# Attention into a feed-forward block: q of batch 1 loaded four tokens to a partition and turned by DMA

## The chip, the cores and the metric

The kernel runs on one core of a Trainium2 chip. The metric is the device time of one execution in microseconds (us). A core has a matrix engine (TensorE, in the profile PE, its weight loads PEld), a vector engine (VectorE, DVE), an engine for activation functions (ScalarE, ACT), a general one (GpSimd, POOL) and one that issues transfers (SyncE, SP). Transfers are carried by 16 DMA engines; POOL issues them on queue q0, SP on queue q1. Tiles lie in SBUF; PE writes to PSUM.

## The reference

Linear attention with a cosine weighting of positions, followed by a feed-forward block with the approximate GELU. q, k and v are 8 batches x 8 heads x 576 tokens x 64, in float32.

```python
def phi(x, c, s):
    r = np.maximum(x, 0.0)
    return np.concatenate([r * c, r * s], axis=-1)   # 64 -> 128 features
q_p, k_p = phi(q, cos_w, sin_w), phi(k, cos_w, sin_w)
kv  = np.einsum('bhsf,bhsd->bhfd', k_p, v)
z   = np.sum(k_p, axis=2)
num = np.einsum('bhsf,bhfd->bhsd', q_p, kv)
den = np.einsum('bhsf,bhf->bhs', q_p, z)[..., None] + 1e-06
x   = (num / den), heads side by side                # 4608 tokens x 512
h   = x @ w_in                                       # 512 x 2048
out = (h * sigmoid(1.702 * h)) @ w_out               # 2048 x 512, float32
```

## The kernel before

The work goes batch by batch. A schedule is written out by hand: each engine works through its instructions in the order of the program, and so do the queues of POOL and SP. A transfer that must wait for its buffer holds up what is issued behind it on its engine.

For one batch the steps are these. `load` brings k and v (and q of batches 0 and 1) as float32 with nine consecutive tokens on a partition and two heads stacked on the partitions (64 partitions each). `load_q` brings q of the other batches with four consecutive tokens on a partition, in two DMAs: 512 tokens on 128 partitions with all heads, and the last 64 tokens on 64 partitions. `trig` (L145 on DVE, L143 on ACT) and `trig_q` (L158) apply the ReLU and the weights of cosine and sine; they write `kr` (k) and `qn0` or `qn` (q, two views of one tile), in bfloat16. q must then be turned so that the 128 features lie on the partitions (`qT`). `qturn_pe` (L174) does it on PE by 128x128 transposes into PSUM, from where `qevac` (L182 on ACT, L184 on DVE) copies them out. `qturn_dma` (L192) does it by a transposing DMA of SP from SBUF to SBUF, one for each of five parts of a batch. `vcopy` (L164, L166) casts v into `vt`, which has a column of ones beside each head for the sum z.

`kv_mm` (L210) computes k^T v with z, `kv_evac` copies it to SBUF, `num_mm` (L223) computes numerators and denominators of 128 tokens, `num_div` (L231, L233, L235 on DVE) divides them into `xn`. x is turned by PE (`xturn_mm` L253, then `xturn_evac` L260 on ACT) in batches 0 and 1 and by DMA (`xturn_dma` L266) from batch 2 on. The PSUM pool of these steps (`at`) has two buffers, which `kv_mm`, `num_mm` and, in batch 1, the turn of q take one after the other; the turn of x writes into the buffer of its numerators, so that a buffer comes free when `xturn_evac` has read it.

The first product (`mm1`, L276) gives 16 blocks of 128 of the 2048 hidden features for 512 tokens, four matmuls each; ACT applies the GELU (L281). The remaining 64 tokens of a batch go through `mm1_tail` (L303) or, for batches 2 to 7 together, `mm1_tails` (L294). The second product (`mm2`, L326) sums over the 16 blocks for a row group of 128 tokens. It is called in parts: `mm2(b, t, lo, hi)` sums blocks lo to hi of row group t; blocks 4g to 4g+3 need the quarter g of w_out. With the last part ACT copies the group out of PSUM (L330) and POOL stores it (L333).

The loads at the start go like this. SP loads k and q of batch 0. POOL loads v of batch 0 and the four parts of w_in, cast to bfloat16 under way, and then k of batch 1, two quarters of w_out, q and v of batch 1 and the other two quarters of w_out. The attention of batch 1 is laid between the parts of the second product of batch 0. From batch 2 on, a loop does the same with the next batch, q turned by DMA.

These functions are touched:

Of the kernel before, what the change touches and what calls it, by code (L numbers as in the profile page):

```python
# [9 lines left out]
F32 = mybir.dt.float32  # L10
BF16 = mybir.dt.bfloat16
# [8 lines left out]
def kernel(  # L20
# [9 lines left out]
    nc = tc.nc  # L30
    B, H, S, D = q.shape
# [4 lines left out]
    NS = S // 64  # L36
    MT = 512
    NI = H // 2
# [7 lines left out]
    pmm = ctx.enter_context(tc.tile_pool(name="pmm", bufs=4, space=PSUM))  # L46
    pat = ctx.enter_context(tc.tile_pool(name="pat", bufs=2, space=PSUM))
# [4 lines left out]
    def raw(name, dt=F32):  # L52
        return one.tile([128, NI, S], dt, name=name)

    def src_of(src, b, i0=0, i1=NI):
        return src[b, 2 * i0:2 * i1].rearrange("(i hh) (p j) d -> (hh p) i (j d)", hh=2, j=NS)

    qf = one.tile([128, 2560], F32, name="qf")
    kf, vf, vb = raw("kf"), raw("vf"), raw("vb", BF16)
    qf0 = qf[:, 0:NI * S].rearrange("p (i e) -> p i e", i=NI)  # L60
    for t, src, cut in ((kf, k, 192), (qf0, q, 256)):
# [34 lines left out]
    qn0 = qn.rearrange("p c h f -> p (c h f)")[:, 0:NS * NI * 128].rearrange(  # L96
        "p (j i f) -> p j i f", j=NS, i=NI)
# [14 lines left out]
    def load(t, src, b, eng=nc.gpsimd):  # L112
        eng.dma_start(out=t, in_=src_of(src, b))

    def load_q(b, eng=nc.sync):
        eng.dma_start(out=qf[:, 0:2048].rearrange("p (h e) -> p h e", h=H),
                            in_=q[b, :, 0:512, :].rearrange("h (p c) d -> p h (c d)", c=4))
        eng.dma_start(out=qf[0:64, 2048:2560].rearrange("p (h e) -> p h e", h=H),
                            in_=q[b, :, 512:S, :].rearrange("h p d -> p h d"))

    def load_win(g):
        nc.gpsimd.dma_start(out=w_in_sb[g], in_=win_r[:, :, ts(g, 512)])

    def load_wout(g):
        nc.gpsimd.dma_start(out=w_out_sb[:, ts(g, 4), :], in_=wout_r[:, g])
# [6 lines left out]
    load_win(1)  # L132
    nc.gpsimd.tensor_copy(gate[0:1, 1:2], vb[0:1, 3, 0:1])
    load_win(2)
    load_win(3)


    def trig(dst, src, j, act=False):
        i = src[:, :, ts(j, 64)]
        for cs, w in enumerate((cosw, sinw)):  # L140
            o = dst[:, j, :, ts(cs, 64)]
            if act:
                nc.scalar.activation(o, i, AF.Relu, scale=w[:, j:j + 1])  # L143
            else:
                nc.vector.tensor_scalar(o, i, 0.0, w[:, j:j + 1], op0=MAX, op1=MUL)  # L145

    def trig_q(c, act=False):
        n = 128 if c < 4 else 64
        if c < 4:
            i = qf[:, 0:2048].rearrange("p (h c d) -> p c h d", h=H, c=4)[:, c]  # L150
        else:
            i = qf[0:64, 2048:2560].rearrange("p (h d) -> p h d", h=H)
        for cs, w in enumerate((cosw, sinw)):
            o, sc = qn[0:n, c, :, ts(cs, 64)], w[0:n, NS + c:NS + c + 1]
            if act:
                nc.scalar.activation(o, i, AF.Relu, scale=sc)
            else:
                nc.vector.tensor_scalar(o, i, 0.0, sc, op0=MAX, op1=MUL)  # L158

    def vcopy(i0, i1, act=False):  # L160
        o = vt[:, :, i0:i1, 0:64].rearrange("p j i e -> p i j e")
        i = vf[:, i0:i1].rearrange("p i (j e) -> p i j e", e=64)
        if act:
            nc.scalar.activation(o, i, AF.Copy)  # L164
        else:
            nc.vector.tensor_copy(o, i)  # L166

    tps = {}

    def qturn_pe(c, home=None):  # L170
        tp = pmm.tile([128, 2, NI, 128], BF16, name="mm") if home is None else home
        for j in range(2 * c, min(2 * c + 2, NS)):
            for i in range(NI):
                nc.tensor.transpose(tp[:, j % 2, i], qn0[:, j, i, :], ident)  # L174
        tps[c] = tp

    def qevac(c, act=False):
        n = min(2 * c + 2, NS) - 2 * c
        o = qT[:, :, ds(c * 128, n * 64)].rearrange("f h (j p) -> f j h p", j=n)
        i = tps.pop(c)[:, 0:n].rearrange("f j i (hh p) -> f j (i hh) p", hh=2)  # L180
        if act:
            nc.scalar.activation(o, i, AF.Copy)  # L182
        else:
            nc.vector.tensor_copy(o, i)  # L184

    def at_homes():
        t = pat.tile([128, 2, 512], F32, name="at")
        return [t[:, u].bitcast(BF16).rearrange("p (j i f) -> p j i f", j=2, i=NI) for u in range(2)]

    def qturn_dma(c):  # L190
        n = 128 if c < 4 else 64
        nc.sync.dma_start_transpose(out=qT[:, :, c * 128:c * 128 + n],  # L192
                                    in_=qn[0:n, c].rearrange("p h f -> p (h f)"))
# [19 lines left out]
    def kv_evac(i0, i1):  # L213
        o = st["kvs"][:, :, i0:i1, 0:65]
        nc.vector.tensor_copy(o, st["ps", i0].rearrange("p hh (i e) -> p hh i e", e=65))  # L215
# [29 lines left out]
    def x_open(b):  # L245
        x[b] = xpool.tile([128, KC, S], BF16, name="xT")

    def xturn_mm(c):
        ps, xn = nums[c]
        xv = xn.rearrange("p a h e -> p (a h e)")  # L250
        for kc in range(KC):
            o = ps[:, kc // 2, ds(264 + (kc % 2) * 64, 64)].bitcast(BF16)
            nc.tensor.transpose(o, xv[:, ts(kc, 128)], ident)  # L253
# [43 lines left out]
    def mm1_tail(b, half):  # L297
        if half == 0 and b % 2 == 0:
            gt[0] = gpool.tile([128, FC, 128], BF16, name="gtail", bufs=2)
        hps = pmm.tile([128, 8, 64], F32, name="mm")  # L300
        for f in range(8):
            for kc in range(KC):
                nc.tensor.matmul(hps[:, f], w_in_of(kc, half * 8 + f), x[b][:, kc, MT:S],  # L303
                                 start=(kc == 0), stop=(kc == KC - 1))
        nc.scalar.activation(gt[0][:, ts(half, 8), ts(b % 2, 64)], hps, AF.Gelu_apprx_sigmoid)

    yp = {}
    out_j = [out[b * S:b * S + S].rearrange("(p j) d -> j p d", j=NS) for b in range(2)]

    def rows(b, t):  # L310

        if t == 4:
            return [(64 * u, 64, out_j[u][NS - 1]) for u in range(2)]
        if t > 4:
            return [(64 * u, 64, out[(w + 1) * S - 64:(w + 1) * S])
                    for u, w in enumerate((TB + 2 * (t - 5), TB + 2 * (t - 5) + 1))]
        if b < 2:
            return [(64 * u, 64, out_j[b][2 * t + u]) for u in range(2)]
        return [(0, 128, out[b * S:b * S + 512].rearrange("(p c) d -> c p d", c=4)[t])]

    def mm2(b, t, lo, hi, c0=0, c1=d_model):
        if lo == 0:
            yp[t, c0] = pmm.tile([128, d_model], F32, name="mm")
        for fc in range(lo, hi):
            w = gT[fc][:, ts(t, 128)] if t < 4 else gt[0][:, fc, :] if t == 4 else gl_t[:, fc, ts(t - 5, 128)]
            nc.tensor.matmul(yp[t, c0][:, c0:c1], w, w_out_sb[:, fc, c0:c1],  # L326
                             start=(fc == 0), stop=(fc == FC - 1))
        if hi == FC:
            ysb = ypool.tile([128, d_model], F32, name="ysb")
            nc.scalar.activation(ysb[:, c0:c1], yp[t, c0][:, c0:c1], AF.Identity)  # L330
            for p0, n, dst in rows(b, t):
                eng = nc.sync if b == B - 1 else nc.gpsimd
                eng.dma_start(out=dst[:, c0:c1], in_=ysb[p0:p0 + n, c0:c1])  # L333
# [81 lines left out]
    start_block(0)  # L415


    load(kf, k, 1)
    load_wout(0)
    load_wout(1)  # L420
    load(qf0, q, 1)
    load(vf, v, 1)
    load_wout(2)
    load_wout(3)
    for j in range(NS):
        trig(kr, kf, j)
# [1 line left out]
        mm1(0, fc)  # L428
    mm1_tail(0, 0)
    mm1_tail(0, 1)  # L430
    for j in range(5):
        trig(qn0, qf0, j)
    for j in range(5, NS):
        trig(qn0, qf0, j, act=True)
    for t in range(4):
        mm2(0, t, 0, 4)
    mm2(0, 0, 4, 8)
    mm2(0, 1, 4, 8)
    ha = at_homes()
    qturn_pe(0, ha[0])  # L440
    qturn_pe(1, ha[1])
    qevac(0)
    qevac(1, act=True)
    mm2(0, 2, 4, 8)
    mm2(0, 3, 4, 8)
    hb = at_homes()
    qturn_pe(2, hb[0])
    qturn_pe(3, hb[1])
    vcopy(0, 2)
    vcopy(2, 4, act=True)  # L450
    qevac(2)
    qevac(3, act=True)
    load_q(2, nc.gpsimd)
    load(kf, k, 2, nc.gpsimd)
    load(vf, v, 2, nc.gpsimd)
    mm2(0, 0, 8, 12)
    mm2(0, 1, 8, 12)
    hc = at_homes()
    qturn_pe(4, hc[0])
    qevac(4)  # L460
    kv_open()
    kv_mm(0, 4, vt_rhs, 0, 65)
    kv_evac(0, 4)
    mm2(0, 2, 8, 12)
    mm2(0, 3, 8, 12)
    num_mm(0)
    num_div(0)
    num_mm(1)
    num_div(1)
    x_open(1)  # L470
    mm2(0, 0, 12, 16)
    mm2(0, 1, 12, 16)
    xturn_mm(0)
    xturn_evac(1, 0)
    mm2(0, 2, 12, 16)
    xturn_mm(1)
    xturn_evac(1, 1)
    num_mm(2)
# [83 lines left out]
```

## Time and profile before

| | |
|---|---|
| median of 3 runs | 295.21 us (295.20 to 295.99) |
| the profiled execution | 295.72 us, its span 294.0 us |
| PE busy | 284.8 us (97%), 2552 instructions |
| DVE, ACT, POOL busy | 126.1, 131.5, 34.7 us |
| TensorE clock granted | 1.00 throughout |
| DMA | 52.38 MB, of it 32.52 MB on q1 (SP) and 19.47 MB on q0 (POOL) |

The busy time of PE is its matmuls and transposes. The share of the DMA is the mean over 16 engines; it can pass 1, where packets of one engine overlap. The chain that ended last is followed back from the last instruction: at each step to what released it, or to the instruction before it on its engine. In the chain's view a row has a start, a length and what ran. The table of windows gives for each stretch of the span the busy time of each engine, the clock and the DMA's share. The DMA view has packets, MB and share of time for each queue, and for each issue the time until its data landed.

### The profile page before, as it was taken

How to read it: one execution, taken by the hardware profiler on the slowest of the kernel's cores; microseconds unless marked ns; L12 is line 12 of the kernel's file. 1: busy time of each engine (PE TensorE's matmuls, PEld its weight loads, DVE VectorE, ACT ScalarE, POOL GpSimd, SP SyncE). 2: the span in 40 equal slices, each digit the busy share in tenths (PEclk: the TensorE clock that was granted, in tenths of full speed). 3: DMA queues.
4: the chain of work that ended last, by engine and by line, in shares of the span. 5: the costliest groups of instructions: out<-in, count | busy, mean ns of one | idle time of the engine just before them, and what ended most of it. 6: DMA issues, size and time to landing. Idle time of an engine off the chain costs nothing.

```text
span 294.0 us, 6250 instructions
## 1 busy us (share of the span) xinstructions
PE 284.8 (97%) x2552; PEld 161.9 (55%) x2587; DVE 126.1 (43%) x362; ACT 131.5 (45%) x230; POOL 34.7 (12%) x68
## 2 busy tenths in 40 slices
PE   8879999999999999999999999999999999999995
PEld 4775656857454555455545554555455545565444
DVE  4674514693264825581567156725763420000000
ACT  7847653685104631463136412651175117773111
POOL 6260031500123001100110011000100010000000
PEclk9999999999999999999999999999999999999999
DMA  7999979596178965797469936995595240000322
GB/s 255 238 222 283 372 192 362 169 139 184 38 139 254 296 182 136 213 311 211 111 199 338 223 90 183 328 221 131 144 371 110 74 116 36 3 0 2 88 90 71
DMA packets 67228, 52.38 MB, mean 178 GB/s; under 512 B 47392, under 2 KB 57376, under 8 KB 67200
## 3 DMA queue, kind: packets, MB, share of 16 engines
q1 hardware_dynamic: 59824, 32.52, 43.2%
q0 software_dynamic: 7376, 19.47, 23.2%
q8 instruction: 20, 0.33, 0.4%
q14 instruction: 8, 0.07, 0.1%
HBM read 36.70 MB, written 9.44 MB: 157 GB/s over the span
## 4 chain that ended last, share of the span: by engine, by line
PE 95%; ACT 1%; issue 1%; DVE 1%; ACTq 0%
PE mm L326 42%; PE mm L276 36%; PE at L210 4%; PE mm L294 4%; PE at L223 3%; PE mm L338 3%; PE mm L303 2%; ACT g L281 1%; PE at L253 1%; DVE xn L235 1%; PE at L174 1%; PE mm L174 1%; DVE inv L233 0%; DVE den L231 0%; ACT ysb L330 0%
## 5 line engine op out<-in xcount | busy, mean ns | idle before, releaser
L326 PE MATMUL mm<-w_out_sb,g 128*128 128x512 bf16 (+1 forms) x506 | 116.2, 372 | 1.3 <-issue 0.2
L276 PE MATMUL mm<-xT,w_in 128*128 128x512 bf16 (+1 forms) x598 | 112.7, 345 | 0.5
L281 ACT ACTIVATE g<-mm 128x512 bf16<-128x512 f32 x128 | 75.6, 598 | 31.9 <-PE mm L276 31.9
L276 PEld LDWEIGHTS <-w_in 128*128 128x128 bf16 x608 | 61.8, 114 | 49.0
L326 PEld LDWEIGHTS <-g 128*128 128x128 bf16 x528 | 48.7, 98 | 49.5
L330 ACT ACTIVATE ysb<-mm 128x512 f32<-128x512 f32 (+1 forms) x37 | 21.7, 586 | 111.4 <-PE mm L326 111.4
L333 POOL DMA_DIRECT2D out_dram<-ysb x38 | 20.7, 548 | 177.2 <-ACT ysb L330 177.1
L145 DVE TENSOR_SCALAR kr<-kf,cosw 128x256 bf16<-128x256 f32 x68 | 23.7, 348 | 27.3 <-DMA kf<-in_k_dram 27.3
L235 DVE TENSOR_TENSOR xn<-at,inv 128x512 bf16<-128x512 f32 x40 | 27.7, 692 | 1.6 <-DVE inv L233 0.2
L145 DVE TENSOR_SCALAR kr<-kf,sinw 128x256 bf16<-128x256 f32 x68 | 23.8, 350 | 0.0
L231 DVE TENSOR_SCALAR den<-at 128x8 f32<-128x8 f32 x40 | 6.7, 166 | 36.9 <-PE at L223 36.9
L215 DVE CAST kvs<-at 128x520 bf16<-128x520 f32 (+1 forms) x9 | 5.8, 642 | 33.1 <-PE at L210 33.0
L223 PEld LDWEIGHTS <-qT 128*128 128x128 bf16 x320 | 14.5, 97 | 7.3
L223 PE MATMUL at<-kvs,qT 128*128 128x65 bf16 x320 | 15.9, 193 | 0.0
L158 DVE TENSOR_SCALAR qn<-qf,sinw 128x512 bf16<-128x512 f32 (+1 forms) x30 | 14.3, 477 | 0.0
L158 DVE TENSOR_SCALAR qn<-qf,cosw 128x512 bf16<-128x512 f32 (+1 forms) x30 | 14.3, 477 | 0.0
L210 PEld LDWEIGHTS <-kr 64*128 64x128 bf16 x648 | 10.2, 94 | 3.5 <-issue 3.2
L294 PE MATMUL mm<-xt,w_in 128*128 128x384 bf16 x64 | 10.6, 326 | 0.0
L326 PE MATMUL mm<-w_out_sb,gl_t 128*128 128x512 bf16 x47 | 10.5, 379 | 0.1
L338 PE MATMUL mm<-warm 128*128 128x64 bf16 (+1 forms) x114 | 8.5, 237 | 1.3 <-DVE warm L76 1.3
L294 PEld LDWEIGHTS <-w_in 128*128 128x128 bf16 x64 | 7.2, 113 | 3.3
L295 ACT ACTIVATE gl_t<-mm 128x384 bf16<-128x384 f32 x16 | 7.9, 491 | 2.4 <-PE mm L294 2.4
(60 smaller groups left out, 122.7 us busy)
## 6 DMA issues: line engine op xcount, KB each, us to landing
kf<-in_k_dram SPq DMA_DIRECT2D x5, 1152.0 KB, 6.5
vf<-in_v_dram SPq DMA_DIRECT2D x5, 1152.0 KB, 9.5
qf<-in_q_dram SPq DMA_DIRECT2D x5, 1024.0 KB, 5.7
out_dram<-ysb POOLq DMA_DIRECT2D x20, 256.0 KB, 2.6
kf<-in_k_dram POOLq DMA_DIRECT2D x2, 1152.0 KB, 10.2
vf<-in_v_dram POOLq DMA_DIRECT2D x2, 1152.0 KB, 13.7
out_dram<-ysb POOLq DMA_DIRECT2D x18, 128.0 KB, 3.2
w_in<-in_moe_w_in_dram POOLq DMA_DIRECT2D x4, 512.0 KB, 9.2
```

The lines of the kernel that those rows point to most:

```text
L145: nc.vector.tensor_scalar(o, i, 0.0, w[:, j:j + 1], op0=MAX, op1=MUL)
L158: nc.vector.tensor_scalar(o, i, 0.0, sc, op0=MAX, op1=MUL)
L210: nc.tensor.matmul(st["kv", i][:, hh, ds(col, n)], kr[r, j, i, :], rhs(r, i, j), start=(j == 0), stop=(j == NS - 1))
L223: nc.tensor.matmul(ps[:, h // 4, ds((h % 4) * 65, 65)], qT[:, h, ts(c, 128)], st["kvs"][:, hh, i, 0:65], start=True, stop=True)
L235: nc.vector.tensor_tensor(xn, pv[:, :, :, 0:64], inv.unsqueeze(3).to_broadcast([128, 2, 4, 64]), op=MUL)
L276: nc.tensor.matmul(hp[fc][:, t0:t1], w_in_of(kc, fc), x[b][:, kc, t0:t1], start=(kc == 0), stop=(kc == KC - 1))
L281: nc.scalar.activation(g, hp.pop(fc), AF.Gelu_apprx_sigmoid)
L294: nc.tensor.matmul(hps, w_in_of(kc, fc), xt[:, kc, :], start=(kc == 0), stop=(kc == KC - 1))
L326: nc.tensor.matmul(yp[t, c0][:, c0:c1], w, w_out_sb[:, fc, c0:c1], start=(fc == 0), stop=(fc == FC - 1))
L330: nc.scalar.activation(ysb[:, c0:c1], yp[t, c0][:, c0:c1], AF.Identity)
L333: eng.dma_start(out=dst[:, c0:c1], in_=ysb[p0:p0 + n, c0:c1])
L338: nc.tensor.matmul(w[:, 0:cols], warm[:, 0:128], warm[:, 0:cols], start=True, stop=True)
```

## The change

The turn of q of batch 1 on PE, with its evictions and its PSUM buffers (`at_homes`), is taken out. q of batch 1 is loaded by `load_q` on POOL, ahead of the fourth part of w_in (the code's part 3); `trig_q` on DVE and `qturn_dma` on SP follow in the program before the remaining loads. The order of these loads becomes w_out 0, k, w_out 1, w_out 2, v, w_out 3. The second product of batch 0 runs through its blocks 0 to 11 without a break; k^T v of batch 1 stands behind them, that is a quarter of the product later, and the last quarter is laid around the numerators and the turn of x in another order. The loads of q and k of batch 2 are issued two thirds into that stretch of the program, v behind the copies of v. Since the tokens of batch 1 now lie four to a partition, the rows of its output are stored as those of later batches are.

```diff
@@ -132,7 +132,6 @@
     load_win(1)
     nc.gpsimd.tensor_copy(gate[0:1, 1:2], vb[0:1, 3, 0:1])
     load_win(2)
-    load_win(3)
 
 
     def trig(dst, src, j, act=False):
@@ -167,8 +166,8 @@
 
     tps = {}
 
-    def qturn_pe(c, home=None):
-        tp = pmm.tile([128, 2, NI, 128], BF16, name="mm") if home is None else home
+    def qturn_pe(c):
+        tp = pmm.tile([128, 2, NI, 128], BF16, name="mm")
         for j in range(2 * c, min(2 * c + 2, NS)):
             for i in range(NI):
                 nc.tensor.transpose(tp[:, j % 2, i], qn0[:, j, i, :], ident)
@@ -182,10 +181,6 @@
             nc.scalar.activation(o, i, AF.Copy)
         else:
             nc.vector.tensor_copy(o, i)
-
-    def at_homes():
-        t = pat.tile([128, 2, 512], F32, name="at")
-        return [t[:, u].bitcast(BF16).rearrange("p (j i f) -> p j i f", j=2, i=NI) for u in range(2)]
 
     def qturn_dma(c):
         n = 128 if c < 4 else 64
@@ -305,17 +300,17 @@
         nc.scalar.activation(gt[0][:, ts(half, 8), ts(b % 2, 64)], hps, AF.Gelu_apprx_sigmoid)
 
     yp = {}
-    out_j = [out[b * S:b * S + S].rearrange("(p j) d -> j p d", j=NS) for b in range(2)]
+    out_j = out[0:S].rearrange("(p j) d -> j p d", j=NS)
 
     def rows(b, t):
 
         if t == 4:
-            return [(64 * u, 64, out_j[u][NS - 1]) for u in range(2)]
+            return [(0, 64, out_j[NS - 1]), (64, 64, out[2 * S - 64:2 * S])]
         if t > 4:
             return [(64 * u, 64, out[(w + 1) * S - 64:(w + 1) * S])
                     for u, w in enumerate((TB + 2 * (t - 5), TB + 2 * (t - 5) + 1))]
-        if b < 2:
-            return [(64 * u, 64, out_j[b][2 * t + u]) for u in range(2)]
+        if b == 0:
+            return [(64 * u, 64, out_j[2 * t + u]) for u in range(2)]
         return [(0, 128, out[b * S:b * S + 512].rearrange("(p c) d -> c p d", c=4)[t])]
 
     def mm2(b, t, lo, hi, c0=0, c1=d_model):
@@ -415,12 +410,16 @@
     start_block(0)
 
 
+    load_q(1, nc.gpsimd)
+    load_win(3)
+    for c in range(5):
+        trig_q(c)
+        qturn_dma(c)
+    load_wout(0)
     load(kf, k, 1)
-    load_wout(0)
     load_wout(1)
-    load(qf0, q, 1)
+    load_wout(2)
     load(vf, v, 1)
-    load_wout(2)
     load_wout(3)
     for j in range(NS):
         trig(kr, kf, j)
@@ -428,51 +427,29 @@
         mm1(0, fc)
     mm1_tail(0, 0)
     mm1_tail(0, 1)
-    for j in range(5):
-        trig(qn0, qf0, j)
-    for j in range(5, NS):
-        trig(qn0, qf0, j, act=True)
+    for g in range(2):
+        for t in range(4):
+            mm2(0, t, 4 * g, 4 * g + 4)
+    load_q(2, nc.gpsimd)
+    load(kf, k, 2, nc.gpsimd)
     for t in range(4):
-        mm2(0, t, 0, 4)
-    mm2(0, 0, 4, 8)
-    mm2(0, 1, 4, 8)
-    ha = at_homes()
-    qturn_pe(0, ha[0])
-    qturn_pe(1, ha[1])
-    qevac(0)
-    qevac(1, act=True)
-    mm2(0, 2, 4, 8)
-    mm2(0, 3, 4, 8)
-    hb = at_homes()
-    qturn_pe(2, hb[0])
-    qturn_pe(3, hb[1])
+        mm2(0, t, 8, 12)
     vcopy(0, 2)
     vcopy(2, 4, act=True)
-    qevac(2)
-    qevac(3, act=True)
-    load_q(2, nc.gpsimd)
-    load(kf, k, 2, nc.gpsimd)
     load(vf, v, 2, nc.gpsimd)
-    mm2(0, 0, 8, 12)
-    mm2(0, 1, 8, 12)
-    hc = at_homes()
-    qturn_pe(4, hc[0])
-    qevac(4)
     kv_open()
     kv_mm(0, 4, vt_rhs, 0, 65)
     kv_evac(0, 4)
-    mm2(0, 2, 8, 12)
-    mm2(0, 3, 8, 12)
+    mm2(0, 0, 12, 16)
     num_mm(0)
     num_div(0)
     num_mm(1)
     num_div(1)
     x_open(1)
-    mm2(0, 0, 12, 16)
     mm2(0, 1, 12, 16)
+    mm2(0, 2, 12, 16)
     xturn_mm(0)
     xturn_evac(1, 0)
-    mm2(0, 2, 12, 16)
     xturn_mm(1)
     xturn_evac(1, 1)
     num_mm(2)
```

## The prediction

> **What bounds the kernel now.** I read the page first, for the busy shares and the chain that ended last:
>
> ```profile
> span 294.0 us, 6250 instructions
> PE 284.8 (97%) x2552; PEld 161.9 (55%) x2587; DVE 126.1 (43%) x362; ACT 131.5 (45%) x230; POOL 34.7 (12%) x68
> PE 95%; ACT 1%; issue 1%; DVE 1%; ACTq 0%
> ```
>
> TensorE (PE) is busy nearly throughout and is 95% of the chain: what leaves PE shortens the kernel, if nothing comes late in its place. So next came the chain in order of time (start, length, what), in the stretch that the change touches:
>
> ```profile
> 41.01 0.89 PE at L174 x16
> 41.90 1.73 PE mm L326 x8
> 43.63 0.89 PE at L174 x16
> ...
> 46.25 0.22 PE at L174 x4
> ...
> 46.49 1.26 PE at L210 x72
> ...
> 49.58 0.48 PE at L223 x16
> 50.07 1.73 PE mm L326 x8
> 51.79 0.22 PE at L253 x4
> 52.02 0.86 PE mm L326 x4
> 52.88 0.22 PE at L253 x4
> 53.10 0.26 PE at L223 x8
> ```
>
> L174 is the turn of q of batch 1 on PE, L210 k^T v, L223 the numerators (num_mm), L253 the turn of x, L326 the second product. No gap of weight stands between them: PE sets the pace.
>
> The turn moves to DMA, so the third view is the DMA's. The table of windows gives its share as 1.02 from 20 to 41 us: in just this stretch the weights and batch 1 are still coming in, one behind the other on POOL's queue (q0). From each load's issue and its time to landing: w_in part 2 lands at 20.5 us, part 3 at 23.1, k at 26.2, w_out 0 and 1 at 28.5 and 31.0, q at 33.8, v at 36.6, w_out 2 and 3 at 39.1 and 41.5. So a w_out quarter takes about 2.45 us of the saturated queue, a w_in quarter 2.6, and q, k or v of a batch 2.9.
>
> How do transposes (SP's queue, q1) fare beside such a stream? Where two queues overlap, the DMA view of a narrow window counts the packets of each. First 123.7 to 124.3 us (stores of the output against loads of SP), then 83.36 to 83.75 and 87.15 to 87.6 us (stores against DMA transposes), and last 62 to 63 us, transposes alone:
>
> ```profile
> q0 software_dynamic: 42, 0.17, 69.6%
> q1 hardware_dynamic: 40, 0.09, 38.8%
> ...
> q0 software_dynamic: 16, 0.07, 116.2%
> q1 hardware_dynamic: 15, 0.00, 4.3%
> ...
> q0 software_dynamic: 16, 0.06, 78.8%
> q1 hardware_dynamic: 14, 0.00, 3.5%
> ...
> q1 hardware_dynamic: 768, 0.19, 104.2%
> ```
>
> Columns: packets, MB, share of 16 engines. In each overlap the queues get one packet each in turn, whatever the size. A transpose packet is 256 bytes, a store's 4 KB: alone the transposes run 768 packets a us, beside stores 15 in 0.39 us. That decides the forecast.
>
> **The removed PE work.** 36 transposes, 0.89 + 0.89 + 0.22 = 2.0 us of the chain, with nothing beside them. Their evictions (three on DVE of 0.69, 0.69 and 0.42 us, two on ACT of 1.02) and ACT's eight scalings of 0.49 us go too; neither engine was waited for there, so no gain. The scalings on DVE become ten of 0.48 us (those of batch 2) instead of ten of 0.35; DVE is idle for 4.15 us waiting for k at that place, and has free stretches after: nothing. The 128-row stores replace pairs of 64-row stores on POOL, off the chain: nothing.
>
> **The loads.** The new order on POOL is w_in 2, q (two DMAs), w_in 3, w_out 0, k, w_out 1, w_out 2, v, w_out 3. q's scalings of batch 0 end near 11.8 us, before POOL reaches the new load (after 14 us), so that wait is free. By the durations above, without transposes: q at 23.7 (2.9 plus 0.3 for the 64-token piece), w_in 3 at 26.3, w_out 0 at 28.8, k 31.7, w_out 1 34.1, w_out 2 36.6, v 39.5, w_out 3 41.9. Needed: w_in 3 by its first use, 24.21 + 28 x 0.216 = 30.3; w_out 0 by 35.8; w_out 1 by 35.83 + 16 x 0.216 = 39.3; w_out 2 by 42.7; k^T v at 46.2, for which k needs 4.7 us of scalings on DVE (18 at an interval of 0.26) and v 1.2 us of copies; w_out 3 at 47.6. The margins are 4 to 7 us. That is the cover; it costs nothing while the stream keeps its pace.
>
> **The queue behind.** The load of q of batch 2 waited on POOL 18.6 us for the ACT scalings, until 39.94. Now its wait is for DVE's ten scalings, 23.8 + 4.0, about 28 us; k of batch 2 waits for the scalings of k (31.7 + 4.7 = 36.4), v of batch 2 for the copies (about 41). All three are issued before the stream has drained, and it runs on without a gap: q2 to 45.1, k2 48.0, v2 50.9. Before, it paused from 41.5 to about 42.
>
> **The DMA transposes.** The first scaling pair takes 0.8 us after q; from SP's issue to the first packets took 1.2 us at 58.95 us, so the first packets are ready at about 25.7 us. Each of four parts has 1024 packets (128 tokens x 1024 x 2 bytes / 256), the last 512. The slots that the stream leaves are its own packets, one for one: 92 in the us from 30 (0.41 MB, 4.5 KB each) and 60 in that from 35 (0.24 MB, 4 KB each) make 256 for a q, k or v (1152 KB) and 128 for a w_out quarter (512 KB). From 26.3 us to the end of v2: 4 x 128 + 5 x 256 + 16 = about 1810, and the tail of w_in 3 adds some 100. Part 0 (1024) is through after v and w_out 3, near 43 us: in time for num_mm(0) at 48.5. Part 1 needs 2048, which is all that the stream has: it lands when the stream ends. That is 50.9, plus 1810/16 = 113 slots x 21 ns (16 engines / 768 a us) = 2.4, so 53.3; the first stores of batch 0 (two of 128 KB) come into the queue at 49 and add about 1 us: **54.3 us**. After it the other parts run free, 1.4 us each, ahead of PE.
>
> PE is at num_mm(1) at 35.83 + 48 x 0.216 + 1.26 + 0.16 + 0.86 + 0.24 = 48.7 us: a wait of 5.6 us. Everything else of PE is queued behind num_mm(1), the rest of the second product included. Bounds: 3.4 us, if some engines drain their share early or v2 is issued late; 9.3, if the load packets themselves slow by 15% beside transposes (24.6 us x 0.15 = 3.7; the store packets' share of 116% at 83 us speaks for some of that). I take 5.6, near the lower end, as the 108% in the 123.7 us window shows little slowing for packets in turn.
>
> The Trainium skill (DMA: Bandwidth & Descriptors, section Queues, rings and completion order) says that an engine takes turns between queues by whole packets of typically 9 to 17 descriptors. The turns agree with the trace; one 256-byte packet a turn in the two overlaps does not show so many descriptors of a transpose in one. By that rule the sum would come out as in the second rival.
>
> **The order of the end.** num_mm(2) takes the PSUM buffer of num 0, which ACT's eviction of xturn(0) frees. Now two row groups of the second product stand ahead of xturn(0), xturn(1) follows at once, and nothing lies between. ACT must first evict the second group (0.60), starts the other 0.49 later (51.83 to 52.32 before) and needs 0.59: free 1.1 us after the product ends, while PE is there after 2 x 0.22 = 0.44. Wait 0.7 us (bounds 0 and 0.8); before, a group of 0.86 covered it.
>
> **The sum.** -2.0 + 0.7 + 5.6 = +4.3 us. The profiled execution took 295.72 us (span 294.0 and 1.7 around it), 0.5 over the median of 295.21: 300.0 for its like, and 299.5 us on the median. The likeliest case's own range is +2 to +8.3: 297.2 to 303.5.
>
> **The rivals.**
> *In time (faster).* If the transposes get three or more packets for one of the stream's, parts 1, 2, 3 and 4 are there at 48.7, 51.8, 53.9 and 54.9 us, when PE asks, and the weights still come in time. Then -2.0 + 0.7 = -1.3: 293.9 us, or 293.2 if the buffer wait does not show. For it: SP's transposes of later batches cost PE nothing. Against: they ran with q0 almost empty, and the two overlaps show one for one. It decides whether 2048 packets are through by 48.7 us. Chance 0.17.
> *Equal shares in time (no change).* If a turn holds some 16 transpose packets (16 x 21 = 0.33 us, as long as a w_out packet), the transposes take half of the engines: 4608/768 = 6.0 us of work, done by 37.7, and each load after it is 6.0 us late. w_out 1 lands at 40.1 against 39.3, a wait of 0.8; v, 45.5 + 1.2, is still in time. -2.0 + 0.7 + 0.8 = -0.5: 294.7 us. It is what the page's rule of whole packets gives. For it: the sum of shares can hold it. Against: the counted packets. Chance 0.09, of which 0.07 within the bound below.
>
> **How the numbers follow.** The starved turn has 0.74. About 0.3% (0.9 us) is what a measurement of this kernel can tell from no change. Slower 0.74 + 0.02 = 0.76, same 0.07, faster 0.17. The range goes from the faster rival's 293.9 to the likeliest case's upper end of 303.5; left out are some 0.05 below and 0.1 above.
>
> **What the changed profile would show.** L174 with 36 fewer in the chain; w_in 3 at about 26 us; five qT transposes on SP that start near 25 us and stretch past 50; q0 without a pause to 51 us or later; one wait of PE ahead of L223 near 49 us, released by a DMA into qT, of 3 to 9 us; a second of 0.7 us after the second L253. I am wrong if the qT transposes land by 48 us, if PE waits ahead of L326 (weights) instead, or if the packets of both queues in 30 to 40 us are far from one for one.

## The result and the profile after

The changed kernel takes 304.39 us in the median of four runs (303.33 to 305.81) against 295.22 us: a ratio of 1.0307 [1.0262, 1.0353]. It is slower by 9.2 us, where 4.3 were forecast and the range ended at 303.5. The profiled execution took 304.52 us, with a span of 302.8 (before 294.0). Lines have moved in the file: the turn of q on PE is now L173, k^T v L205, num_mm L218, the turn of x L248 and its eviction L255, the tail of the first product L298, the second product L321, the stores L328, the DMA turn of q L187.

From the page, as before: span, busy PE and the chain by engine. The chain now holds 10% of DMA:

```profile
span 302.8 us, 6202 instructions
PE 288.3 (95%) x2551; PEld 161.4 (53%) x2551; DVE 125.9 (42%) x359; ACT 126.4 (42%) x220; POOL 33.5 (11%) x65
PE 87%; DMA 10%; DVE 1%; issue 1%; ACT 0%; ACTq 0%
```

In the chain in order of time, a single DMA, part 1 of qT, stands where the removed transposes were:

```profile
26.15 30.03 DMA qT<-qn
56.18 0.05 issue
56.23 0.62 PE at L218 x8
56.85 3.43 PE mm L321 x8
...
60.79 0.60 ACT xT L255
...
61.44 0.49 PE at L218 x8
```

It was issued at 26.15 us and landed 30.03 us later; the five of batch 2 took 3.3 us in the median before. The DMA view of 32 to 35 us shows why (packets, MB, share of 16 engines):

```profile
q0 software_dynamic: 160, 0.59, 95.9%
q1 hardware_dynamic: 160, 0.04, 9.9%
```

160 packets of the loads and 160 of the transposes, in a stretch in which the two queues had nothing but loads and transposes. Equal counts alone would also fit turns of many packets on both sides. A shorter view, of 32 to 32.35 us, is about as long as one load packet of 4 KB (0.32 us) and one transpose together:

```profile
q0 software_dynamic: 16, 0.06, 86.4%
q1 hardware_dynamic: 16, 0.00, 8.6%
```

That is one of each for 16 engines. From 29 to 50 us there are 1462 packets of q0 and 1463 of q1, and for 1453 of the transposes the trace has a packet of q0 that starts 4 ns before the transpose ends. So a turn is one packet. At 53 a us the transposes move at 7% of the 768 that they reached alone from 62 to 63 us in the kernel before.

The timeline of PE, with the start, the length and in brackets the wait ahead of the row, has the wait at num_mm(1), and two things behind it:

```profile
48.96 0.41 PE L218 MATMUL at<-kvs,qT 128*128 128x65 bf16 x8
56.23 0.62 PE L218 MATMUL at<-kvs,qT 128*128 128x65 bf16 x8 [6.86 <-DMA qT<-qn]
56.66 3.60 PE L321 MATMUL mm<-w_out_sb,g 128*128 128x512 bf16 x8
60.06 1.06 PE L248 MATMUL at<-ident,xn 128*128 128x128 bf16 x8
61.44 0.49 PE L218 MATMUL at<-kvs,qT 128*128 128x65 bf16 x8 [0.32 <-ACT xT L255]
```

The 0.32 us ahead of the last row is what is left of the wait for the PSUM buffer. The new thing is the pace: eight matmuls of the second product took 3.43 us in the chain, where they took 1.73 before. The table of windows (columns: window, length, busy PE, PEld, DVE, ACT, POOL, then the granted clock, the DMA's share and GB/s) shows it:

```profile
50.00:51.00 1.00, 0.00 (x0) 0.00 (x0) 0.54 (x1) 0.00 (x0) 0.95 (x2) 1.00 1.12 435
51.00:52.00 1.00, 0.00 (x0) 0.00 (x0) 0.00 (x0) 0.00 (x0) 0.15 (x1) 0.72 1.44 184
52.00:53.00 1.00, 0.00 (x0) 0.00 (x0) 0.00 (x0) 0.00 (x0) 0.00 (x0) 0.50 0.55 204
...
60.00:61.00 1.00, 1.00 (x9) 0.90 (x8) 0.00 (x0) 0.70 (x2) 0.53 (x2) 0.50 0.52 111
61.00:62.00 1.00, 0.68 (x12) 0.44 (x10) 0.03 (x1) 0.88 (x2) 0.81 (x2) 0.66 0.70 152
62.00:63.00 1.00, 1.00 (x11) 0.66 (x10) 0.93 (x3) 0.17 (x1) 0.23 (x1) 1.00 0.63 139
```

About 2 us into the idle time the clock fell to 0.50, and it was full again only between 61 and 62 us, more than 5 us after PE had resumed. The Trainium skill (TensorE: Matmul & The Clock Gate, section Why this matters for your kernels) warns of gaps of more than about 3 us between matmuls for this reason; the trace agrees for this gap of 6.86 us, and the forecast had left it out.

To compare kernels, one stretch is measured throughout: from the first tail matmul of batch 0 (L298, before L303) to num_mm(2) in PE's timeline. Its ends in the kernel before, and its start in the changed one, are these rows:

```profile
33.54 2.29 PE L303 MATMUL mm<-xT,w_in 128*128 128x64 bf16 x64
52.97 0.40 PE L223 MATMUL at<-kvs,qT 128*128 128x65 bf16 x8
...
34.31 2.30 PE L298 MATMUL mm<-xT,w_in 128*128 128x64 bf16 x64
```

It runs from 33.54 to 52.97 us before, 19.43 us, and from 34.31 to 61.44 after, 27.13 us: 7.70 us more. Of the 8.8 us between the spans, 0.8 lie ahead of the stretch and 0.3 behind it.

### The profile page after: what moved, and what is told of

It reads as the page before. It is cut to its first block, busy times and chain, and to the rows that moved or that the text cites. A ratio compares the mean times of both kernels' runs of the same rounds, so it can differ in the third digit from the quotient of the medians.

```text
span 302.8 us, 6202 instructions
## 1 busy us (share of the span) xinstructions
PE 288.3 (95%) x2551; PEld 161.4 (53%) x2551; DVE 125.9 (42%) x359; ACT 126.4 (42%) x220; POOL 33.5 (11%) x65
## 4 chain that ended last, share of the span: by engine, by line
PE 87%; DMA 10%; DVE 1%; issue 1%; ACT 0%; ACTq 0%
PE mm L321 38%; PE mm L271 34%; DMA qT<-qn 10%; PE mm L289 3%; PE at L218 3%; PE at L205 3%; PE mm L333 3%; PE mm L298 1%; DVE xn L230 1%; PE mm L173 1%; PE at L248 1%; DVE inv L228 0%; ACT xT L255 0%; DVE den L226 0%; ACT ysb L325 0%
## 5 line engine op out<-in xcount | busy, mean ns | idle before, releaser
L321 PE MATMUL mm<-w_out_sb,g 128*128 128x512 bf16 (+1 forms) x528 | 119.0, 376 | 0.0
L321 PEld LDWEIGHTS <-g 128*128 128x128 bf16 x528 | 49.2, 98 | 51.2 <-issue 1.6
L328 POOL DMA_DIRECT2D out_dram<-ysb x34 | 18.4, 542 | 190.1 <-ACT ysb L325 190.1
L218 PE MATMUL at<-kvs,qT 128*128 128x65 bf16 x320 | 16.4, 195 | 7.2 <-DMA qT<-qn 6.9
L218 PEld LDWEIGHTS <-qT 128*128 128x128 bf16 x320 | 14.9, 99 | 14.8 <-DMA qT<-qn 7.0
L157 DVE TENSOR_SCALAR qn<-qf,cosw 128x512 bf16<-128x512 f32 (+1 forms) x35 | 16.7, 477 | 0.9 <-DMA qf<-in_q_dram 0.9
L157 DVE TENSOR_SCALAR qn<-qf,sinw 128x512 bf16<-128x512 f32 (+1 forms) x35 | 16.7, 478 | 0.0
L205 PEld LDWEIGHTS <-kr 64*128 64x128 bf16 x648 | 10.1, 94 | 3.8 <-issue 3.6
L165 DVE CAST vt<-vf 128x2304 bf16<-128x2304 f32 (+1 forms) x7 | 8.9, 1269 | 4.3 <-DMA vf<-in_v_dram 4.3
L289 PE MATMUL mm<-xt,w_in 128*128 128x384 bf16 x64 | 10.6, 326 | 0.0
L321 PE MATMUL mm<-w_out_sb,gl_t 128*128 128x512 bf16 x48 | 10.5, 379 | 0.0
L333 PE MATMUL mm<-warm 128*128 128x64 bf16 (+1 forms) x115 | 9.3, 249 | 1.3 <-DVE warm L76 1.3
```

Of the source, the lines that this page charges most:

```text
L205: nc.tensor.matmul(st["kv", i][:, hh, ds(col, n)], kr[r, j, i, :], rhs(r, i, j), start=(j == 0), stop=(j == NS - 1))
L218: nc.tensor.matmul(ps[:, h // 4, ds((h % 4) * 65, 65)], qT[:, h, ts(c, 128)], st["kvs"][:, hh, i, 0:65], start=True, stop=True)
L289: nc.tensor.matmul(hps, w_in_of(kc, fc), xt[:, kc, :], start=(kc == 0), stop=(kc == KC - 1))
L333: nc.tensor.matmul(w[:, 0:cols], warm[:, 0:128], warm[:, 0:cols], start=True, stop=True)
```

## The experiments

The theory to be tested: the queues get one packet each in turn, whatever its size, and because POOL's loads of batch 2 go on without a pause, part 1 of qT lands when that stream ends. Then PE's idle time costs again through the clock. The rivals: the transposes are slow of themselves, the bytes ahead of them decide, or loads or weights in their new order are late.

### The loads of batch 2 behind the transposes, on SP

```diff
-    load_q(2, nc.gpsimd)
-    load(kf, k, 2, nc.gpsimd)
+    load_q(2)
+    load(kf, k, 2, nc.sync)
...
-    load(vf, v, 2, nc.gpsimd)
+    load(vf, v, 2, nc.sync)
```

> The changed kernel with the loads of q, k and v of batch 2 issued by SP instead of POOL, so behind the transposes of batch 1 on the same queue. Theory (one packet each in turn beside the stream of loads, so the transposes end when the stream ends): the stream on q0 now ends with the last quarter of w_out near 44 us; part 1 of qT lands near 46 us and the last part near 50, PE does not wait at num_mm(1), its clock stays 1.00; about 294 to 295 us. Rival (transposes are slow of themselves beside anything, or the bytes ahead of them decide): part 1 still lands after 53 us, PE waits 4 to 7 us, 301 to 304 us.

294.79 us, ratio 0.9967 [0.9948, 0.9987]. The wait is gone (num_mm(0) and (1) are one row of 16 in PE's timeline), and part 1 landed near 45.6 us, 10.6 us earlier:

```profile
48.97 0.65 PE L218 MATMUL at<-kvs,qT 128*128 128x65 bf16 x16
49.45 1.89 PE L321 MATMUL mm<-w_out_sb,g 128*128 128x512 bf16 x8
51.18 0.86 PE L248 MATMUL at<-ident,xn 128*128 128x128 bf16 x8
52.52 0.40 PE L218 MATMUL at<-kvs,qT 128*128 128x65 bf16 x8 [0.48 <-ACT xT L255]
```

From 44 to 46 us the DMA view counts 1812 transposes against 2 packets of q0. So the transposes are not slow of themselves, and the wait hangs on the stream that goes on. The stretch is 18.20 us, 1.2 less than before. The 0.48 us at the end is the buffer wait.

### Only v of batch 2 held back

```diff
-    load(vf, v, 2, nc.gpsimd)
+    load(vf, v, 2, nc.sync)
```

> The changed kernel with only the load of v of batch 2 moved to SP, behind the transposes. Theory: the stream on q0 ends one load earlier, with k of batch 2 near 51 us; part 1 of qT lands some 3 to 4 us earlier, at 52 to 53 us, PE waits about 3 us instead of 6.9 and spends a shorter time at half clock: 298 to 300 us. Rival (the end of the stream does not decide): part 1 stays near 56 us, 304 us.

300.74 us, 1.0145 [1.0103, 1.0187]. One load less in the stream, and the wait shrinks from 6.86 to 4.25 us, with part 1 there at 52.8:

```profile
52.84 0.51 PE L218 MATMUL at<-kvs,qT 128*128 128x65 bf16 x8 [4.25 <-DMA qT<-qn]
53.17 3.50 PE L321 MATMUL mm<-w_out_sb,g 128*128 128x512 bf16 x8
```

The landing comes 3.4 us earlier for a load of 2.9 us, as the theory has it; 0.3 of the 3.4 is an earlier issue of the first transpose (24.42 against 24.71). The wait is longer than the 3 us expected, and the time lies just above the 298 to 300. The second product behind it is slow here too, but the clock fell later than in the changed kernel:

```profile
50.00:52.00 2.00, 0.00 (x0) 0.00 (x0) 0.00 (x0) 0.00 (x0) 0.38 (x1) 1.00 1.71 110
52.00:54.00 2.00, 1.16 (x10) 0.61 (x11) 0.53 (x3) 0.00 (x0) 0.00 (x0) 0.75 0.91 216
54.00:56.00 2.00, 2.00 (x6) 0.73 (x5) 0.53 (x1) 0.60 (x1) 0.01 (x1) 0.50 1.01 230
```

The mean of 0.75 is a fall at 53.0 us, 4.4 us after the last matmul and when PE had already resumed. From num_mm(1) to num_mm(2) the run takes 57.84 - 52.84 = 5.00 us all the same, 1.7 more than at the full clock (3.3, next but one experiment).

### The change without its turn

```diff
     for c in range(5):
         trig_q(c)
-        qturn_dma(c)
```

> The changed kernel with the five transposing DMAs of batch 1 left out (its numerators are made from the turned q of batch 0). This gives the change without its wait. Theory: 2.0 us less of PE work, 0.7 us of wait for the PSUM buffer at num_mm(2), no other wait: about 294 us. Rival (the loads in their new order are late as well): PE waits ahead of the second product or of k^T v, 295 us or more.

295.02 us, 0.9968 [0.9954, 0.9983], the stretch 33.81 to 52.01, 18.20 us: the same as with the loads behind the transposes. No wait for weights, k or v appears ahead of L321 or L205. The time is a microsecond above the forecast and at the rival's bound, but the waits that the rival needs aren't there. What the change would give without its wait is therefore 1.2 us in the stretch, and some 0.9 us in the medians.

### PE kept at work during the wait

```diff
     num_div(0)
+    idle(26)
     num_mm(1)
```

> The changed kernel with 26 matmuls of 512 columns on zeros (5.6 us) between num_mm(0) and num_mm(1), in the time in which PE waits. Theory (the idle time costs a second time, because the granted clock falls to 0.50 and stays there for 5 us after it): the transposes land as before near 56 us, the clock stays 1.00 and the second product behind it runs at 0.216 us a matmul instead of 0.43: 2 us less, about 302 us. Rival (that stretch is slow because of DMA or ACT): still 304 us.

The four runs are 302.23, 302.54, 305.52 and 306.46 us, a ratio of 1.0295 [1.0222, 1.0367]: against the changed kernel the time doesn't tell them apart, and the median of 304.03 is what the rival expected. The profiled execution (302.54 us) tells it. The clock is 1.00 through the whole stretch:

```profile
50.36 5.77 PE L333 MATMUL mm<-warm 128*128 128x512 bf16 x26 [0.44 <-ACT ysb L325]
56.21 0.42 PE L218 MATMUL at<-kvs,qT 128*128 128x65 bf16 x8
56.47 1.89 PE L321 MATMUL mm<-w_out_sb,g 128*128 128x512 bf16 x8
...
59.53 0.40 PE L218 MATMUL at<-kvs,qT 128*128 128x65 bf16 x8 [0.73 <-ACT xT L255]
```

From num_mm(1) to num_mm(2) it is 59.53 - 56.21 = 3.32 us here and 61.44 - 56.23 = 5.21 in the changed kernel: the lowered clock cost 1.9 us. Part 1 landed at 56.2 in both. In the two long runs the mean clock was 0.994 instead of 0.999; they have no trace, and whether the transposes landed later there than the matmuls reached is not known.

### The order at the end

The first experiment, with row group 2 of the second product back between the two turns of x:

```diff
     mm2(0, 1, 12, 16)
-    mm2(0, 2, 12, 16)
     xturn_mm(0)
     xturn_evac(1, 0)
+    mm2(0, 2, 12, 16)
     xturn_mm(1)
```

> The changed kernel with the loads of batch 2 on SP, as in the first run, and with row group 2 of the second product back between the two turns of x, as in the kernel before. Theory: the wait of 0.5 to 0.7 us at num_mm(2) for the PSUM buffer is gone, and nothing comes late in its place: 2.0 us less PE work than before and no wait, 0.7 us less than the first run, a ratio to before of 0.993 to 0.995. Rival (that wait has another cause, or ACT is late elsewhere): as the first run, 0.997.

294.08 us, 0.9922 [0.9905, 0.9939]. The stretch is 35.03 to 52.62, 17.59 us, 0.6 less than without this edit, and num_mm(2) no longer waits for ACT:

```profile
51.30 0.40 PE L248 MATMUL at<-ident,xn 128*128 128x128 bf16 x4
51.53 1.03 PE L321 MATMUL mm<-w_out_sb,g 128*128 128x512 bf16 x4
52.40 0.39 PE L248 MATMUL at<-ident,xn 128*128 128x128 bf16 x4
52.62 0.41 PE L218 MATMUL at<-kvs,qT 128*128 128x65 bf16 x8
```

This version beats both kernels, the one before by 0.8%.

### Twice the packets for the same elements

```diff
+    kb = raw("kb", BF16)
...
-    load(kf, k, 1)
+    load(kb, k, 1)
...
-    load(vf, v, 1)
+    load(vb, v, 1)
```

and the same for batch 2, with the steps that read them.

> The changed kernel with k and v of batches 1 and 2 cast to bfloat16 by their loads, in the same order on POOL: their packets are then 1152 bytes, 512 a load instead of 256, and by the pace of the loads of v of batch 0 a load takes about as long. Theory (one transpose packet for each packet of the stream, whatever its size): by 50 us the stream has given 400 turns more, part 1 of qT (2048 packets) lands near 50 us instead of 56, while parts 2 to 4 still wait for the end of the stream; PE waits under 2 us at num_mm(1) and 2 to 3 at num_mm(2): 299 to 302 us. Rival (the end of the stream, or the bytes ahead, decide for every part): part 1 lands at 55 us or later and the time stays near 304 us.

307.72 us in two runs, 1.039 [1.0365, 1.0415]: a miss. Part 1 landed at 56.2, not near 50. Until 50 us the DMA view counts 1710 transpose packets (1487 in the changed kernel): 223 turns more, not 400. The DMA view of 48 to 51 us shows which half of the expectation failed:

```profile
q0 software_dynamic: 299, 0.47, 91.0%
q1 hardware_dynamic: 299, 0.08, 35.8%
```

One for one holds with the small casting packets (most of the 299 of q0) as it does with large ones. But the turns came at 100 a us, where the casting load of w_in alone made 197 (window of 17 to 18 us before), so that the stream took longer too: taking turns slowed such packets by much more than the 21 ns of a transpose. As parts 2, 3 and 4 were late as well, PE waited four times, 8.6 us in all, and once 0.6 us for the last quarter of w_out. The late landing of part 1 looks like the rival. But v of batch 2, the last of the loads, came much later:

```profile
47.88 0.75 POOL L114 DMA_DIRECT2D vb<-in_v_dram  x1 [6.84 <-ACT vt L164]
vb<-in_v_dram POOLq DMA_DIRECT2D x1, 576.0 KB, 15.4
```

With 15.4 us from its issue to landing it was there at 63.3 us, 7 us after part 1. So the end of the stream doesn't decide for every part: a part lands when it has had its turns, and in the changed kernel part 1 needs about all that the stream has.

### The removed work alone

The kernel before without `qturn_pe` and `qevac` of batch 1:

```diff
-    ha = at_homes()
-    qturn_pe(0, ha[0])
-    qturn_pe(1, ha[1])
-    qevac(0)
-    qevac(1, act=True)
...
-    hc = at_homes()
-    qturn_pe(4, hc[0])
-    qevac(4)
```

> The kernel before with the 36 transposes of q of batch 1 on PE and their five evictions left out (the numerators of batch 1 are made from the turned q of batch 0). This prices the removed work alone. Theory: PE is the bound there and nothing else is late, so 2.0 us less, a ratio of 0.993. Rival (something else ends just behind PE, and part of the 2.0 us was never to be had): 0.996 or more.

293.26 us, 0.9908 [0.9892, 0.9923], the stretch 33.32 to 50.65, 17.33 us: 2.1 less than before. The work was on the path in full. In the medians it is 2.7 us; the 0.6 beyond the stretch isn't accounted for.

### Held back, but on POOL

The first experiment had moved the loads to another queue as well. Here they stay on POOL and wait for the last part of qT, and row group 2 stands between the turns:

```diff
+    nc.gpsimd.tensor_copy(gate[0:1, 2:3], qT[0:1, 0, 512:513])
     load_q(2, nc.gpsimd)
     load(kf, k, 2, nc.gpsimd)
```

> The changed kernel with the loads of batch 2 still on POOL, but held back there by a one-element copy that reads the last turned part of q of batch 1, and with row group 2 back between the two turns of x. The queue is that of the changed kernel, only the stream has an end before part 1. Theory (the stream that goes on decides, not the queue that carries it): as the run with these loads on SP and that order, part 1 lands near 46 us, no wait of PE, a ratio to before of 0.992 to 0.995. Rival (loads on POOL are what slows SP's transposes, or the loads of batch 2 now come late for PE): part 1 after 50 us, or a wait of DVE for q of batch 2 that reaches PE, 297 us or more.

293.91 us, 0.9947 [0.9928, 0.9967], the stretch 17.60 us, as with the loads on SP. POOL waited for the transposes, and PE no longer does:

```profile
50.14 0.17 POOL L433 CAST gate<-qT 1x1 f32<-1x1 bf16 x1 [25.32 <-DMA qT<-qn]
50.69 0.91 POOL L116 DMA_DIRECT2D qf<-in_q_dram  x1 [0.38 <-DVE xn L230]
```

So the unbroken stream decides, not the queue that carries it, and q, k and v of batch 2 are still in time when they start at 50 us. It beats both kernels too; from the version with SP the intervals don't tell it.

## Why the prediction was right and wrong

**The mechanism** was the one forecast: one packet in turn, part 0 in time (45.5 us, forecast near 43), part 1 with the end of the stream, one wait of PE at num_mm(1), everything else of PE behind it. The counts, 160 and 160 and 16 and 16, and the runs that cut the stream short show it.

**The removed work**, 2.0 us by the chain, is 2.1 us in the stretch. **The loads**: all weights, k and v came in time, as worked out. **The end of batch 0**, 0.7 us, is 0.6 (17.59 against 18.20). With both, the change without its wait is at -1.2 us in the stretch; -1.3 was forecast.

**The wait** was mis-sized: 5.6 us were taken, 7.0 measured (56.23 less 49.2, where num_mm(0) ended), inside its bounds of 3.4 to 9.3. The term said that part 1 lands at 54.3; it landed at 56.2. Three pieces of that term were too good. The first transpose packet came 1.2 us after SP's issue before; here the view of 26 to 28 us still has 144 packets of q0 and none of q1, and the first come after 28 us, so more than two us of turns were lost at the start and had to be made up at the end. From 51 to 53 us q0 moved 80 packets where 92 a us is its pace for such loads: 15 packets that start between 51.1 and 51.6 us took over 1 us each, others beside them 0.18. The only packet of the instruction queue q8 in that stretch starts 0.6 us ahead of them, and three of the other runs (v held back, PE kept at work, casting loads) show long packets of one or the other queue behind such a packet too; whether the one causes the other no run shows. And the engines didn't end together, as the sum had them do: from 53 to 56 us, with the stream nearly over, the transposes ran at 1029 packets in 3 us, not at 768 a us. In the trace 2048 of them, as many as parts 0 and 1 hold, had started by 54.2 us, which is close to the forecast 54.3; but part 1 landed only at 56.2, when 2696 had. Some engines were on later parts while others still had packets of part 1, and a part lands with its last engine.

**The step that failed** is one that isn't in the sum: a wait of PE was priced at its length alone. The idle time cost another 1.9 us at half clock. The stretch then adds up: -1.2 + 7.0 + 1.9 = 7.7, as measured. Of the 4.9 us between the 4.3 forecast and the 9.2 measured, 1.9 are this step and 1.4 the size of the wait; 1.1 lie outside the stretch, 0.4 is that the execution profiled before was 0.5 us above its median and the one after 0.1, and 0.1 is the removed work with the buffer wait.

**The rest**, 0.8 us ahead of the stretch, was there before anything of the change runs on PE: the first 112 matmuls, which only warm PE up, took 7.71 us in the profile before, 8.51 in the one after, and 6.96 in that with the loads held on POOL, though the programs don't differ up to there. In each trace these matmuls start at half pace (0.427 us for 512 columns, 0.216 later), and the full pace comes at 5.4, 7.1 and 3.9 us; half of the 1.65 us between the first two is the 0.8. The Trainium skill (TensorE: Matmul & The Clock Gate, section What's actually happening) calls the moment at which the clock opens dependent on a free-running window; the trace agrees in that it differs between executions. It is part of the spread, as is perhaps the 0.3 us behind the stretch, and it puts some tenths of the 9.2 us outside the change; how much in the median isn't shown, since only one execution of each kernel has a trace.

Of the rivals, *in time* was wrong because nothing gave the transposes more than one packet in turn; with the stream cut the transposes were in time, and the stretch gained 1.2 us where that rival had 1.3. *Equal shares* is refuted by the counts wherever loads and transposes filled the two queues: a turn of a transpose was one packet of 256 bytes. The Trainium skill (DMA: Bandwidth & Descriptors, section Queues, rings and completion order) gives turns of several descriptors; for these transposes the counts differ from it, and they decide.

## What to carry to other kernels

Before work is moved from a busy engine to a DMA, count the packets of the queues that run at that time: against a saturated stream of 4 KB packets a transfer in 256-byte packets gets one in turn, and if it needs as many turns as the stream has packets, it ends when the stream does. Let the stream end first: hold back what isn't needed yet, behind the small transfer on its own queue or behind a gate. And price a wait of PE, where it is the bound, higher than its length: after waits of 4.25, 5.96 and 6.86 us the matmuls behind it ran at half clock here, for 3.4 to 5.4 us. Shorter waits weren't tried.

## What the runs showed of the hardware

- A first transpose packet came 1.2 us after its issue with idle queues, and only at 28.5 us, 3.8 us after an issue at 24.71, beside a full stream.
- A stream of mostly casting packets (1152 bytes) took its turns with transposes at 100 a us, packets of about 4 KB (0.59 MB in 160) at 53. Without loads beside them the transposes ran at 768 a us in the view of 62 to 63 us before, and at 1152 from 45 to 46 us in the run with the loads on SP.
- The granted clock fell to 0.50 at 2.1 us after PE's last matmul in the changed kernel, at 4.4 us with v held back and at 4.6 us with the casting loads, so no fixed delay can be read from these runs. It was full again 3.6 to 5.4 us after the matmuls had resumed.
